# Five groups computed plainly and two pairs by seven products, instead of three and three, in a linear-attention and gated-MLP kernel

## The chip, the cores and the metric

The kernel runs on one core of one Trainium2 chip. The metric is the device time of one execution in microseconds. Three executions of the kernel before took 922.75, 929.16 and 931.92 us, median 929.16 us.

## What is computed

Inputs q, k and v have the shape 8 batches x 8 heads x 576 positions x 64, and `w_in` is 512 x 2048 and `w_out` 2048 x 512, all float32. The reference is:

```python
q_s = softmax(q, axis=-1); k_s = softmax(k, axis=2)      # sums + 1e-9
kv = np.einsum('bhsd,bhse->bhde', k_s, v)
x  = np.einsum('bhsd,bhde->bhse', q_s, kv)               # -> 4608 x 512
h  = x @ w_in                                            # 4608 x 2048
out = (h * np.cos(h)) @ w_out                            # 4608 x 512
```

## The kernel before, in words

**Tokens.** The 576 positions of each batch are cut into 512 and 64. The first 512 of batch b are group b (0 to 7); the eight remainders of 64 together are group 8. So the MLP runs over nine groups of 512 tokens, and over 16 blocks f of 128 columns of `w_in`.

**Precision.** A float32 operand is split into a high and a low part of a reduced type, and a product is three matmuls: high x high, high x low, low x high. A first-layer result h of one group and one f (128 x 512) therefore takes 4 chunks x 3 = 12 matmuls of 128x128 by 128x512 (`unit1`, L839), and the second layer of one group and one f takes 4 row blocks x 3 = 12 more, added into four `acc` banks (`unit2`, L923). Between the two stand the gating, h*cos(h), in four steps (`gated`: turns on ACT L864, rest on DVE L868, cos on ACT L874, gate on DVE L879), and the split of the result (`split_g`: ACT L895, DVE L899). The first six units use plain float32 in the second layer (L916).

**Plain groups and pairs.** Groups below `std` (3) are computed this plain way, 16 units each; the rest, (3,4), (5,6) and (7,8), are taken in pairs by a seven-product scheme (`pair`, `block`, L1152). For a pair and two neighbouring f, the four results (two groups x two f) come from seven products of 6 matmuls each, instead of 4 x 12 = 48 matmuls. The scheme needs sums and differences of x (`x_sums`: L1064, L1075, L1079) and of the weights (`sums`: L998 to L1009, computed once, written to the DRAM tensor `w_sums`, and loaded again for each block of each pair by four GpSimd DMAs, L1127). Within a block the products go to two PSUM banks, `z` and `a` (products 0, 2, 4, 6 to z; 1, 3, 5 to a), and intermediate sums are copied and added into SBUF cells `c` by ACT (L1166) and DVE (L1173). Only the last product's result is gated straight from the bank z.

**PSUM.** There are eight banks: h x 2, acc x 4, att x 2. In a plain group h alternates between the two h banks. In a block z alternates between the two h banks from block to block, and `a` is always the bank `att` 1.

**Attention.** It goes by batch b and by pairs p of heads (`k_steps`: the kv product, L599; `q_steps`; `x_steps`: two matmuls of 128x128 by 128x288 in plain float32, L712, into two banks `xo`). For b below `std` the two use both att banks, and x stays in SBUF (ACT L726 and L729, DVE L737). From `std` on, `spare()` gives `att` 0 alone, since `a` lives in `att` 1: both matmuls go to the same bank, each is copied by ACT (`x_row`, L742) into one row buffer `xs`, and the row is written to the DRAM tensor `x_main`, from which `x_sums` loads it. The softmax steps that matter below are the exponentials on ACT (`q_exp` L653, `k_exp` L561). Exp and sin need different activation tables, each loaded by an instruction on ACT.

**Order.** Nothing waits by hand. `Plan` collects every step with its engine, its assumed duration, what it reads and writes and a due time; `order()` list-schedules them (ACT, DVE, PE, POOL, SP, and the buses of the DMAs) and the instructions are issued on each engine's queue in the order found. The engines then run in order, and semaphores follow from the data. `CFG["spans"]` says over which units of the plain groups the attention of a later batch is to be spread; `CFG["tables"]` = 0 means that the planner gives table loads no time. SP issues all plain DMAs, GpSimd the loads of `w_sums`.

Of the kernel before, what the change touches and what calls it, by code (L numbers as in the profile page):

```python
# [43 lines left out]
    att1=(5.98, 6.97),  # L44
    std=3,
    spans={2: (15.0, 28.0), 3: (24.0, 38.0), 4: (32.0, 47.0)},
    phi=0.906,
# [9 lines left out]
    rounds=8,  # L57
    tables=0,
    alpha=1.33,
# [3 lines left out]
class Plan:  # L63
# [6 lines left out]

    LAT = {("POOL", "SWB"): 0.3, ("ACT", "PE"): 0.37, ("DVE", "PE"): 0.3, ("DVE", "ACT"): 0.14, ("DVE", "DVE"): 0.13,
           ("PE", "PE"): 0.07, ("SP", "SP"): 0.0, ("SP", "BUS"): 0.2}

    def __init__(self):
        self.steps = []
        self.writer, self.readers = {}, {}

    def add(self, eng, us, fn, reads=(), writes=(), due=None, table=None, after=0.0):
# [18 lines left out]
    def load(self, us, fn, reads=(), writes=(), due=None, after=0.0, parts=1, seq=()):  # L97

        t = object()
        self.add(  # L100
            "SP", 0.65 * parts, fn, reads=reads, writes=[*writes, t, *seq], due=due, after=after
        )
        self.add("BUS", us, None, reads=[*reads, t], writes=writes)

    def cast_load(self, us, fn, reads=(), writes=(), due=None):

        t = object()
        self.add("POOL", 1.1, fn, reads=reads, writes=[*writes, t], due=due)
        self.add("SWB", us, None, reads=[*reads, t], writes=writes)

    def lat(self, i, j):

        a, b = self.steps[i], self.steps[j]
        return self.LAT.get((a[0], b[0]), 1.0 if a[0] in ("BUS", "SWB") else 0.2)

    def run(self, edges, prio, release=None, tables=False):
# [14 lines left out]
        for _ in range(n):  # L131
            best = None
            for e in engines:
                if can[e]:
                    t = free[e]
                elif wait[e]:
                    t = max(free[e], wait[e][0][0])
                else:
                    continue
                if best is None or t < best[0]:  # L140
                    best = (t, e)
            t, e = best
            w, c = wait[e], can[e]
            while w and w[0][0] <= t:
                at, i = heappop(w)
                heappush(c, (at if e in ("BUS", "SWB") else prio[i], i))
# [57 lines left out]
def linear_attention_then_cos_gated_mlp(  # L204
# [18 lines left out]
    nc = tc.nc  # L223
# [47 lines left out]
    def v_frame(t):  # L271
# [17 lines left out]
    w_rows = dr.tile([NF, P, DM], F32, name="w_rows")  # L289
    w_sums = dr.tile([NF // 2, P, 7, 2, 2 * P], F32, name="w_sums")  # L290

# [4 lines left out]
    BUFS = dict(  # L296
        x4k=8, kq=2, qm=1, qs=2, ql=1, mt=1, m1=1, m=2, r=2, kvw=4, xs=1, stage=2, wc=2, r2=3, ghi=2,
        glo=2, h=2, acc=4, att=2, qb=1, qf=2, qd=2, sr=5, c=4,
    )
# [18 lines left out]
    for tag, size in (  # L318
# [4 lines left out]
        ("r2", TB), ("ghi", TB), ("glo", TB), ("stage", TB), ("wc", 2 * DM),  # L323
        ("kvw", P), ("mt", 4 * P), ("m1", 2 * P), ("m", 2 * P), ("xs", S), ("kq", 4 * NC * D), ("qb", S), ("qf", S),
    ):
# [255 lines left out]
    def spare(tag, b):  # L581

        return ring(tag) if tag != "att" or b < CFG["std"] else (tag, 0)

# [89 lines left out]
    def x_steps(b, p, place, kvw, tq, tx, due_q, due_x):  # L674
# [7 lines left out]
        slot = ring("x4k") if keep else None  # L682
        xr, xs = quarters(slot), ring("xs")
        cols = [slice(0, HALF), slice(HALF, TB)]
# [89 lines left out]
        cold = 2.0 if b == 0 and p < CFG["cold"] else 1.0  # L774
        qf = ring("qf")
        if blocks:
# [209 lines left out]
    def sums(n):  # L986

        f = 2 * n
        s, hs, ls = ring("wc"), ("x4k", 2 + 2 * (n % 2)), ("x4k", 3 + 2 * (n % 2))

# [16 lines left out]
        def lo():  # L1007
            t = T["sl", n] = sbt([P, 2 * DM], F32R, ls, f"sl_{n}")
            nc.vector.tensor_sub(  # L1009
                t, T["sum", n].rearrange("p f d -> p (f d)"), T["sh", n].bitcast(F32)  # L1010
            )

        def put(i):
            t = T["sh" if i == 0 else "sl", n].bitcast(F32).rearrange("p (s d) -> p s d", s=4)
# [8 lines left out]
        plan.load(0.73 * 2, rows, reads=[("rows", f), ("rows", f + 1)], writes=[s])  # L1023
        plan.add("DVE", 1.5, adds, writes=[s])
        plan.add("ACT", 1.1, hi, reads=[s], writes=quarters(hs))
        plan.add("DVE", 1.22, lo, reads=[s, *quarters(hs)], writes=quarters(ls))
        plan.load(1.0, lambda: put(0), reads=quarters(hs), writes=[("sums", n, 0)], parts=2)
        plan.load(1.0, lambda: put(1), reads=quarters(ls), writes=[("sums", n, 1)], parts=2)
        plan.load(
            2.2, own, reads=[("w", "i", f), ("w", "i", f + 1)], writes=[("sums", n, 2)], parts=3,  # L1030
            due=when(20 + 2.5 * n),
        )


    ORDER = ("11", "5", "6", "3", "7", "2", "4")
    XAT = {0: (2, 3), 1: (4, 5), 6: (6, 7)}
# [10 lines left out]
    def x_sums(k, b1, b2):  # L1047
# [6 lines left out]
        for c in range(2):  # L1054
# [34 lines left out]
            for i, m, sub in (  # L1089
                (0, A0, None),  # L1090
                (1, A0, (A0, A1, A0)),
                (2, A0, (A0, B1, A0)),
                (3, B1, None),
                (4, A1, (A1, B1, A1)),
                (5, B0, None),
                (6, B0, (B0, B0, A0)),
# [6 lines left out]
                xp = x_places(i, c)  # L1103
                plan.add("ACT", 0.62, lambda i=i, m=m, hi=hi: hi(i, m), reads=at(m) + [st[m[0]]], writes=xp)
                plan.add("DVE", 0.69, lambda i=i, m=m, lo=lo: lo(i, m), reads=at(m) + [st[m[0]]], writes=xp)
# [6 lines left out]
    def block(k, n, b1, b2, flip, due):  # L1112

        z, aux = ring("h"), ("att", 1)
        c1, c5, c2 = (ring("c") for _ in range(3))
# [3 lines left out]
        for m in range(4):  # L1119
            place = wide(ring("sr")[1])  # L1120

            def load(m=m, place=place):
                e = min(2 * m + 2, 7)
                t = sbt([P, e - 2 * m, 2, 2 * P], F32R, f"wi{place[2]}", f"s_{k}_{n}_{m}")
                for i in range(2 * m, e):
                    T["s", k, n, i] = t[:, i - 2 * m]
                nc.gpsimd.dma_start(t, w_sums[n, :, 2 * m : e])  # L1127

            plan.cast_load(
                2.0 if m < 3 else 1.2, load, reads=[("sums", n, i) for i in range(3)],  # L1130
                writes=[place, (place, 0), (place, 1)],
# [25 lines left out]
        def pe(i, to, first=False):  # L1157
            plan.add(
                "PE", us, lambda: product(i, to, first),
                reads=[*x_places(i, 0), *x_places(i, 1), ws[i // 2]],  # L1160
                writes=[z if to == "z" else aux], due=due + i * us * CFG["phi"],
            )
# [47 lines left out]
        pe(5, "a", True)  # L1210
        add("a", c1)
        G[b1, f] = post(2, b1, f, c1)
        pe(6, "z")
# [139 lines left out]
    for u in range(NU + 2):  # L1353
        if u >= 2:
            unit2(u - 2, order[u - 2], G.pop(u - 2), when(u + 0.4))
        if u < NU:
            b, f = order[u][:2]
            prepare("i", f)
            if b not in X:
# [57 lines left out]
```

## Time and profile before

| what | value |
|---|---|
| three executions | 922.75, 929.16, 931.92 us |
| profiled execution | 923.85 us, of which the span from the first to the last instruction is 921.8 us |
| granted TensorE clock, mean | 0.987 of full speed |
| busy: PE, PEld, DVE, ACT, POOL | 859.0, 677.9, 617.6, 546.0, 88.6 us |
| first-layer matmuls of plain groups (L839) | 576, from 37.7 to 352.5 us |
| matmuls of the seven-product blocks (L1152) | 1008, from 357.3 to 891.4 us |

Busy times are sums over the span; an engine's share says nothing of which wait ends last, so idle times with their releasers and stretches of the timeline are needed beside them. A matmul's own duration (389 ns for 128x512) is longer than the distance to the next one in a row, because matmuls are pipelined; the pace is read from rows that merge several.

### The profile page before, as it was taken

What the parts mean: (1) busy time and instruction counts of PE and PEld (TensorE: products, weight loads), DVE (VectorE), ACT (ScalarE), POOL (GpSimd) and SP (SyncE); (2) the same over time, 40 slices, a digit from 0 to 9 for tenths busy, and PEclk for the clock granted to TensorE, in tenths of its full rate; (3) what the DMA queues carried; (4) which work ended last, traced back from release to release, by engine and by line L of the source; (5) the groups of instructions that cost most, each with busy time, mean ns of one, the idle gap of its engine ahead of it and who ended that gap; (6) DMA issues with size and microseconds to landing.
All of it is one profiled execution on the core that took longest, in us unless ns stands there. A gap on an engine that the chain in (4) does not pass through costs nothing.

```text
span 921.8 us, 12171 instructions
## 1 busy us (share of the span) xinstructions
PE 859.0 (93%) x4144; PEld 677.9 (74%) x4144; DVE 617.6 (67%) x995; ACT 546.0 (59%) x910; POOL 88.6 (10%) x181
## 2 busy tenths in 40 slices
PE   6889999999898989889899989979999999999998
PEld 4556777877676777668687768757788788878876
DVE  7778889978666967678266757875345666534552
ACT  3798797766555565666446665754445655543541
POOL 1200100100100002012001101100000011100100
PEclk8799999999999999999999999999999999999999
DMA  8993599828579874697349457866324447342312
GB/s 216 340 281 126 170 349 269 229 79 225 131 245 291 204 230 120 178 241 193 120 104 240 121 188 198 212 149 150 101 81 126 148 140 215 101 130 74 98 31 83
DMA packets 209981, 159.67 MB, mean 173 GB/s; under 512 B 115200, under 2 KB 176128, under 8 KB 209920
## 3 DMA queue, kind: packets, MB, share of 16 engines
q1 hardware_dynamic: 196096, 114.86, 44.8%
q0 software_dynamic: 13824, 44.05, 17.6%
q8 instruction: 33, 0.54, 0.2%
q14 instruction: 28, 0.23, 0.1%
HBM read 111.94 MB, written 46.92 MB: 172 GB/s over the span
## 4 chain that ended last, share of the span: by engine, by line
PE 48%; DMA 9%; ACT 6%; DVE 5%; issue 4%; SPq 3%; POOL 0%; ACTq 0%; DVEq 0%; POOLq 0%
PE acc L923 25%; PE z L1152 10%; PE a L1152 7%; PE h L839 4%; DMA q<-in_q_dram 3%; PE x_False L712 2%; DMA s<-w_sums 1%; DMA out_dram<-o 1%; SPq L490 1%; SPq L486 1%; PE kv L599 1%; ACT xs L742 1%; DMA w_sums<-sl 1%; DVE xs L1079 1%; DVE qm L646 1%
## 5 line engine op out<-in xcount | busy, mean ns | idle before, releaser
L1152 PE MATMUL z<-xs,s 128*128 128x512 f32 x576 | 148.3, 395 | 3.0 <-DVE kt L879 1.0
L839 PE MATMUL h<-x,w_i 128*128 128x512 f32 x576 | 143.8, 399 | 4.7 <-DVE kt L879 3.3
L839 PEld LDWEIGHTS h<-x,w_i 128*128 128x128 f32 x576 | 107.4, 189 | 30.7 <-DVE kt L879 5.5
L1152 PEld LDWEIGHTS z<-xs,s 128*128 128x128 f32 x576 | 108.1, 189 | 27.9 <-DVE c L1173 2.5
L1152 PE MATMUL a<-xs,s 128*128 128x512 f32 x432 | 113.2, 398 | 4.6 <-ACT c L1166 4.0
L923 PE MATMUL acc<-w_o,ghi 128*128 128x512 f32 x336 | 108.1, 403 | 1.7 <-DVE o L961 1.1
L1152 PEld LDWEIGHTS a<-xs,s 128*128 128x128 f32 x432 | 81.5, 190 | 23.5 <-ACT c L1166 5.0
L1127 POOL DMA_DIRECT2D s<-w_sums x96 | 50.9, 531 | 415.4 <-PE a L1152 271.2
L923 PEld LDWEIGHTS acc<-w_o,ghi 128*128 128x128 f32 x336 | 62.3, 188 | 16.4 <-DVE o L961 1.9
L712 PE MATMUL x_False<-qf,kvw 128*128 128x288 f32 x128 | 45.6, 444 | 28.7 <-ACT xs L742 24.4
L923 PE MATMUL acc<-w_o,glo 128*128 128x512 f32 x168 | 65.8, 391 | 0.4 <-DVE glo L899 0.4
L712 PEld LDWEIGHTS x_False<-qf,kvw 128*128 128x128 f32 x128 | 22.7, 197 | 43.3 <-ACT xs L742 32.9
L1173 DVE TENSOR_TENSOR c<-a,c 128x512 f32<-128x512 f32 x48 | 33.1, 689 | 22.6 <-PE a L1152 22.2
L864 ACT ACTIVATE stash<-c 128x512 int32<-128x512 f32 x36 | 22.7, 632 | 39.5 <-DVE c L1173 39.2
L864 ACT ACTIVATE kt<-h 128x512 int32<-128x512 f32 x48 | 28.5, 594 | 29.0 <-PE h L839 26.5
L1166 ACT COPY c<-z 128x512 f32<-128x512 f32 x48 | 28.1, 586 | 25.7 <-PE z L1152 25.4
L868 DVE SCALAR_TENSOR_TENSOR kt<-kt,h 128x512 f32<-128x512 int32 x48 | 32.6, 681 | 11.3 <-ACT kt L864 11.3
L874 ACT ACTIVATE kt<-kt 128x512 f32<-128x512 f32 x48 | 30.3, 633 | 15.9 <-DVE kt L868 15.5
L874 ACT ACTIVATE stash<-stash 128x512 f32<-128x512 f32 x48 | 30.3, 631 | 13.5 <-DVE stash L868 13.4
L646 DVE TENSOR_REDUCE qm<-q 128x18 f32<-128x1152 f32 x16 | 21.6, 1350 | 24.4 <-DMA q<-in_q_dram 24.4
L879 DVE TENSOR_TENSOR kt<-kt,h 128x512 f32<-128x512 f32 x42 | 28.6, 680 | 13.6 <-ACT kt L874 13.4
L923 PEld LDWEIGHTS acc<-w_o,glo 128*128 128x128 f32 x168 | 31.5, 188 | 7.7 <-DVE glo L899 0.9
(872 smaller groups left out, 1763.3 us busy)
## 6 DMA issues: line engine op xcount, KB each, us to landing
s<-w_sums POOLq DMA_DIRECT2D x72, 512.0 KB, 4.4
q<-in_q_dram SPq DMA_DIRECT2D x32, 256.0 KB, 5.4
raw_i<-in_moe_w_in_dram SPq DMA_DIRECT2D x16, 512.0 KB, 5.9
raw_o<-in_moe_w_out_dram SPq DMA_DIRECT2D x16, 512.0 KB, 6.4
out_dram<-o SPq DMA_DIRECT2D x32, 256.0 KB, 2.9
v_sb<-in_v_dram SPq DMA_DIRECT2D x30, 256.0 KB, 4.4
k<-in_k_dram SPq DMA_DIRECT2D x14, 512.0 KB, 5.2
qb<-q_rows SPq DMA_DIRECT2D x96, 72.0 KB, 3.2
```

Of the source, the lines that this page charges most:

```text
L646: nc.vector.tensor_reduce(out=m, in_=rows(), axis=AX.X, op=ALU.max)
L712: nc.tensor.matmul(t[:, 0:HALF], T["kv", b, p], T["qf", b, p][:, cs], start=True, stop=not again)
L839: nc.tensor.matmul(o, a, x, start=(c == 0 and n == 0), stop=(c == KC - 1 and n == 2))
L864: nc.scalar.activation(t.bitcast(I32), src(), AF.Identity, bias=0.25, scale=1.0 / TWO_PI)
L868: nc.vector.scalar_tensor_tensor(t, t.bitcast(I32), -TWO_PI, src(), op0=ALU.mult, op1=ALU.add)
L874: nc.scalar.activation(t, t, AF.Sin, bias=0.5 * math.pi)
L879: nc.vector.tensor_mul(o, t, src())
L923: nc.tensor.matmul(T["acc", j], a[:, js], w, start=(first and n == 0), stop=(last and n == 2))
L1127: nc.gpsimd.dma_start(t, w_sums[n, :, 2 * m : e])
L1152: nc.tensor.matmul(o, a, x, start=(first and c == 0 and m == 0), stop=(c == 1 and m == 2), skip_group_check=not first,)
L1166: "ACT", 0.6, lambda: nc.scalar.copy(cell(place), T["z" + to, k, n]),
L1173: lambda: nc.vector.tensor_add(cell(place), T["z" + to, k, n], cell(place)),
```

## The change

`std` becomes 5: groups 0 to 4 are plain, and the pairs are (5,6) and (7,8). The attention of each batch is spread over other units, up to batch 6. `spare()` gives both att banks to all batches, and the blocks use the two h banks alone: z in h bank n % 2 and `a` in the other. The products are issued in the order 0, 5, 2, 1, 4, 3, 6, with the loads of their weights regrouped to match. `w_sums` holds only the four sums; the unchanged parts of `w_in` are kept in a second tensor `w_own`. The low parts of the sums are computed in place. The row buffers `qf` x 2 and `xs` become one ring `row` x 3. The planner gives a table load its time, counts DMAs from batch 2 on 1.3 times as long, and treats GpSimd's loads as users of the same bus as the others.

```diff
 CFG = dict(
-    std=3,
-    spans={2: (15.0, 28.0), 3: (24.0, 38.0), 4: (32.0, 47.0)},
+    std=5,
+    slow=1.3,
+    spans={2: (15.0, 28.0), 3: (29.0, 42.0), 4: (43.0, 56.0), 5: (52.0, 66.0), 6: (62.0, 77.0)},
...
-    tables=0,
+    tables=1.0,
...
-    w_sums = dr.tile([NF // 2, P, 7, 2, 2 * P], F32, name="w_sums")
+    w_sums = dr.tile([NF // 2, P, 4, 2, 2 * P], F32, name="w_sums")
+    w_own = dr.tile([NF, P, 2, DM], F32, name="w_own")
...
     def spare(tag, b):
-        return ring(tag) if tag != "att" or b < CFG["std"] else (tag, 0)
+        return ring(tag)
...
-        xr, xs = quarters(slot), ring("xs")
+        xr = quarters(slot)
...
-        qf = ring("qf")
+        qf, xs = ring("row"), ring("row")
...
     def sums(n):
-        s, hs, ls = ring("wc"), ("x4k", 2 + 2 * (n % 2)), ("x4k", 3 + 2 * (n % 2))
+        s, hs = ring("wc"), ("x4k", 2 + n % 4)
+        due = when((CFG["std"] - 1) * NF + 1.7 * n)
...
-            nc.sync.dma_start(w_sums[n, :, 2:5, i], t[:, 0:3])
-            nc.sync.dma_start(w_sums[n, :, 1, i], t[:, 3])
-
-        def own():
-            for x, k, at in ((f, 0, 0), (f, 1, 5), (f + 1, 1, 6)):
-                t = T["w", "i", x].bitcast(F32)
-                nc.sync.dma_start(w_sums[n, :, at], t[:, :, k * 2 * P : (k + 1) * 2 * P])
+            nc.sync.dma_start(w_sums[n, :, :, i], t)
+
+        def own(x, k):
+            nc.sync.dma_start(w_own[x, :, :, k * 2 * P :], T["w", "i", x].bitcast(F32)[:, :, k * 2 * P :])
...
-    ORDER = ("11", "5", "6", "3", "7", "2", "4")
+    ORDER = (0, 5, 2, 1, 4, 3, 6)
+    TILE = (0, 1, 1, 2, 2, 0, 3)
...
     def block(k, n, b1, b2, flip, due):
-        z, aux = ring("h"), ("att", 1)
+        z, aux = ("h", n % 2), ("h", 1 - n % 2)
...
         pe(0, "z", True)
         copy("z", c1)
+        pe(5, "a", True)
+        add("a", c1)
+        G[b1, f] = post(2, b1, f, c1)
+        pe(2, "z")
+        copy("z", c2)
         pe(1, "a", True)
         copy("a", c5)
-        pe(2, "z")
-        copy("z", c2)
+        pe(4, "z")
+        add("z", c5)
+        G[b2, f + 1] = post(1, b2, f + 1, c5)
         pe(3, "a")
         add("a", c2)
         G[b2, f] = post(0, b2, f, c2)
-        pe(4, "z")
-        add("z", c5)
-        G[b2, f + 1] = post(1, b2, f + 1, c5)
-        pe(5, "a", True)
-        add("a", c1)
-        G[b1, f] = post(2, b1, f, c1)
         pe(6, "z")
         G[b1, f + 1] = post(3, b1, f + 1, z)
...
-            if u == 2 * NF:
+            if u == (STD - 1) * NF:
                 for n in range(NF // 2):
                     sums(n)
```

## Rows read from the trace of the kernel before

**Rows 1.** The page: busy us of each engine, share of the span, instructions.

```profile
PE 859.0 (93%) x4144; PEld 677.9 (74%) x4144; DVE 617.6 (67%) x995; ACT 546.0 (59%) x910; POOL 88.6 (10%) x181
```

**Rows 2.** PE's waits, whole span: waiting line, releaser, total us, times, longest.

```profile
PE x_False L712 <- ACT xs L742: 24.4, 20, 2.9
PE a L1152 <- ACT c L1166: 4.0, 2, 3.1
PE h L839 <- DVE kt L879: 3.3, 4, 1.6
PE acc L923 <- ACT o L964: 2.3, 4, 0.9
PE kv L599 <- DMA v_sb<-in_v_dram: 1.4, 1, 1.4
PE z L1152 <- DVE kt L879: 1.0, 1, 1.0
```

**Rows 3.** Stretches: busy us of PE, PEld, DVE, ACT, POOL, then PEclk, DMA share, GB/s.

```profile
248.20:352.70 104.50, 94.30 (x465) 73.52 (x463) 74.78 (x121) 56.99 (x88) 5.31 (x13) 1.00 0.79 227
772.00:890.00 118.00, 117.23 (x517) 96.68 (x517) 62.08 (x95) 57.06 (x97) 10.56 (x20) 1.00 0.34 96
```

**Rows 4.** The chain of waits: a first-layer unit; one product of a block.

```profile
350.14 2.73 PE h L839 x12
419.21 1.36 PE z L1152 x6
```

**Rows 5.** Timeline of PE, two attention matmuls of batch 5: start us, us.

```profile
406.65 0.65 PE L712 MATMUL x_False<-qf,kvw 128*128 128x288 f32 x2
406.92 0.85 PE L923 MATMUL acc<-w_o,ghi_('s', 0, 0, 3)_3693 128*128 128x512 f32 x2
...
412.98 0.75 PE L712 MATMUL x_False<-qf,kvw 128*128 128x288 f32 x2 [2.92 <-ACT xs L742]
413.35 1.76 PE L1152 MATMUL z<-xs,s 128*128 128x512 f32 x6
```

**Rows 6.** Timeline of ACT across the same wait.

```profile
409.15 1.28 ACT L653 ACT_TABLE_LOAD   x1
410.44 1.16 ACT L653 ACTIVATE q<-q 128x1152 f32<-128x1152 f32 x1
411.51 0.61 ACT L864 ACTIVATE kt_('s', 0, 2, 2)_3858<-c 128x512 int32<-128x512 f32 x1
...
412.54 0.39 ACT L742 COPY xs<-x_False 128x288 f32<-128x288 f32 x1
```

**Rows 7.** Timeline of PE, attention of batch 2, which has both banks.

```profile
172.55 1.13 PE L712 MATMUL x_False<-qf,kvw 128*128 128x288 f32 x4
173.31 3.15 PE L839 MATMUL h<-x,w_i 128*128 128x512 f32 x12
```

**Rows 8.** Timeline of PE and DVE: last product, then z's gate, blocks 0, 7, 19, 23.

```profile
377.61 2.88 PE L1152 MATMUL z<-xs,s 128*128 128x512 f32 x12
390.99 0.69 DVE L879 TENSOR_TENSOR kt_('s', 0, 0, 3)_3619<-kt_('s', 0, 0, 3)_3619,z 128x512 f32<-128x512 f32 x1 [2.15 <-ACT kt_('s', 0, 0, 3)_3619 L874]
...
549.64 1.52 PE L1152 MATMUL z<-xs,s 128*128 128x512 f32 x6
565.33 0.68 DVE L879 TENSOR_TENSOR stash<-stash,z 128x512 f32<-128x512 f32 x1
...
802.40 1.52 PE L1152 MATMUL z<-xs,s 128*128 128x512 f32 x6
805.98 0.69 DVE L879 TENSOR_TENSOR kt_('s', 2, 3, 3)_6957<-kt_('s', 2, 3, 3)_6957,z 128x512 f32<-128x512 f32 x1 [0.70 <-ACT kt_('s', 2, 3, 3)_6957 L874]
...
890.22 1.52 PE L1152 MATMUL z<-xs,s 128*128 128x512 f32 x6
894.29 0.69 DVE L879 TENSOR_TENSOR stash<-stash,z 128x512 f32<-128x512 f32 x1 [1.19 <-ACT stash L874]
```

**Rows 9.** Groups by line: ACT's largest group of table loads.

```profile
L874 ACT ACT_TABLE_LOAD x26 | 33.4, 1283 | 0.5
```

More of the change, by code (lines that the diff above doesn't have):

```diff
@@ L63 @@
 class Plan:
-    LAT = {("POOL", "SWB"): 0.3, ("ACT", "PE"): 0.37, ("DVE", "PE"): 0.3, ("DVE", "ACT"): 0.14, ("DVE", "DVE"): 0.13,
+    LAT = {("POOL", "BUS"): 0.5, ("ACT", "PE"): 0.37, ("DVE", "PE"): 0.3, ("DVE", "ACT"): 0.14, ("DVE", "DVE"): 0.13,
            ("PE", "PE"): 0.07, ("SP", "SP"): 0.0, ("SP", "BUS"): 0.2}
@@ L76, in __init__ @@
         self.writer, self.readers = {}, {}
+        self.slow = 1.0
     def add(self, eng, us, fn, reads=(), writes=(), due=None, table=None, after=0.0):
@@ L100, in load @@
         self.add(
-            "SP", 0.65 * parts, fn, reads=reads, writes=[*writes, t, *seq], due=due, after=after
+            "SP", 0.65 * self.slow * parts, fn, reads=reads, writes=[*writes, t, *seq], due=due, after=after
         )
-        self.add("BUS", us, None, reads=[*reads, t], writes=writes)
+        self.add("BUS", self.slow * us, None, reads=[*reads, t], writes=writes)
     def cast_load(self, us, fn, reads=(), writes=(), due=None):
         t = object()
-        self.add("POOL", 1.1, fn, reads=reads, writes=[*writes, t], due=due)
-        self.add("SWB", us, None, reads=[*reads, t], writes=writes)
+        self.add("POOL", 0.6, fn, reads=reads, writes=[*writes, t], due=due)
+        self.add("BUS", self.slow * us, None, reads=[*reads, t], writes=writes)
     def lat(self, i, j):
         a, b = self.steps[i], self.steps[j]
-        return self.LAT.get((a[0], b[0]), 1.0 if a[0] in ("BUS", "SWB") else 0.2)
+        return self.LAT.get((a[0], b[0]), 1.0 if a[0] == "BUS" else 0.2)
     def run(self, edges, prio, release=None, tables=False):
@@ L145, in run @@
                 at, i = heappop(w)
-                heappush(c, (at if e in ("BUS", "SWB") else prio[i], i))
+                heappush(c, (at if e == "BUS" else prio[i], i))
             i = heappop(c)[1]
@@ L296, in linear_attention_then_cos_gated_mlp @@
     BUFS = dict(
-        x4k=8, kq=2, qm=1, qs=2, ql=1, mt=1, m1=1, m=2, r=2, kvw=4, xs=1, stage=2, wc=2, r2=3, ghi=2,
-        glo=2, h=2, acc=4, att=2, qb=1, qf=2, qd=2, sr=5, c=4,
+        x4k=8, kq=2, qm=1, qs=2, ql=1, mt=1, m1=1, m=2, r=2, kvw=4, row=3, stage=2, wc=2, r2=3, ghi=2,
+        glo=2, h=2, acc=4, att=2, qb=1, qd=2, sr=5, c=4,
     )
@@ L323, in linear_attention_then_cos_gated_mlp @@
         ("r2", TB), ("ghi", TB), ("glo", TB), ("stage", TB), ("wc", 2 * DM),
-        ("kvw", P), ("mt", 4 * P), ("m1", 2 * P), ("m", 2 * P), ("xs", S), ("kq", 4 * NC * D), ("qb", S), ("qf", S),
+        ("kvw", P), ("mt", 4 * P), ("m1", 2 * P), ("m", 2 * P), ("row", S), ("kq", 4 * NC * D), ("qb", S),
     ):
@@ L1007, in lo @@
         def lo():
-            t = T["sl", n] = sbt([P, 2 * DM], F32R, ls, f"sl_{n}")
-            nc.vector.tensor_sub(
-                t, T["sum", n].rearrange("p f d -> p (f d)"), T["sh", n].bitcast(F32)
-            )
-        def put(i):
-            t = T["sh" if i == 0 else "sl", n].bitcast(F32).rearrange("p (s d) -> p s d", s=4)
-            nc.sync.dma_start(w_sums[n, :, 2:5, i], t[:, 0:3])
-            nc.sync.dma_start(w_sums[n, :, 1, i], t[:, 3])
-        def own():
-            for x, k, at in ((f, 0, 0), (f, 1, 5), (f + 1, 1, 6)):
-                t = T["w", "i", x].bitcast(F32)
-                nc.sync.dma_start(w_sums[n, :, at], t[:, :, k * 2 * P : (k + 1) * 2 * P])
@@ L1023, in sums @@
[L1023 to L1032, printed above, removed]
@@ L1035, in linear_attention_then_cos_gated_mlp, with put @@
-    ORDER = ("11", "5", "6", "3", "7", "2", "4")
+            t = T["sum", n].rearrange("p f d -> p (f d)")
+            nc.vector.tensor_sub(t, t, T["sh", n].bitcast(F32))
+        def put(i):
+            if i == 0:
+                t = T["sh", n].bitcast(F32).rearrange("p (s d) -> p s d", s=4)
+            else:
+                t = T["sum", n].rearrange("p f (k d) -> p (f k) d", k=2)
+            nc.sync.dma_start(w_sums[n, :, :, i], t)
+        def own(x, k):
+            nc.sync.dma_start(w_own[x, :, :, k * 2 * P :], T["w", "i", x].bitcast(F32)[:, :, k * 2 * P :])
@@ new lines, in sums @@
+        plan.load(0.73 * 2, rows, reads=[("rows", f), ("rows", f + 1)], writes=[s], due=due)
+        plan.add("DVE", 1.8, adds, writes=[s])
+        plan.add("ACT", 1.1, hi, reads=[s], writes=quarters(hs))
+        plan.add("DVE", 1.22, lo, reads=quarters(hs), writes=[s])
+        plan.load(1.46, lambda: put(0), reads=quarters(hs), writes=[("sums", n, 0)])
+        plan.load(1.46, lambda: put(1), reads=[s], writes=[("sums", n, 1)])
+        for k in range(2):
+            plan.load(
+                1.46 - 0.73 * k, lambda k=k: own(f + k, k), reads=[("w", "i", f + k)], writes=[("own", f + k)],
+                due=when((CFG["std"] - 2.5 + 0.18 * n) * NF),
+            )
@@ L1090, in x_sums @@
                 (0, A0, None),
+                (5, B0, None),
                 (1, A0, (A0, A1, A0)),
                 (2, A0, (A0, B1, A0)),
+                (4, A1, (A1, B1, A1)),
                 (3, B1, None),
-                (4, A1, (A1, B1, A1)),
-                (5, B0, None),
                 (6, B0, (B0, B0, A0)),
@@ L1103, in x_sums @@
                 xp = x_places(i, c)
-                plan.add("ACT", 0.62, lambda i=i, m=m, hi=hi: hi(i, m), reads=at(m) + [st[m[0]]], writes=xp)
+                plan.add(
+                    "ACT", 0.62, lambda i=i, m=m, hi=hi: hi(i, m), reads=at(m) + [st[m[0]]],
+                    writes=xp + [("xw", i)],
+                )
                 plan.add("DVE", 0.69, lambda i=i, m=m, lo=lo: lo(i, m), reads=at(m) + [st[m[0]]], writes=xp)
@@ L1122, in load @@
             def load(m=m, place=place):
[L1123 to L1127, printed above, removed]
+                shape = ([P, 2, DM], [P, 2, 2, 2 * P], [P, 2, 2, 2 * P], [P, 2, 2 * P])[m]
+                t = sbt(shape, F32R, f"wi{place[2]}", f"s_{k}_{n}_{m}")
+                if m == 0:
+                    T["s", k, n, 0], T["s", k, n, 5] = t[:, :, 0 : 2 * P], t[:, :, 2 * P : DM]
+                    src = w_own[f]
+                elif m == 3:
+                    T["s", k, n, 6] = t
+                    src = w_own[f + 1, :, :, 2 * P : DM]
+                elif m == 1:
+                    T["s", k, n, 2], T["s", k, n, 1] = t[:, 0], t[:, 1]
+                    src = w_sums[n, :, 0:4:3]
+                else:
+                    T["s", k, n, 3], T["s", k, n, 4] = t[:, 0], t[:, 1]
+                    src = w_sums[n, :, 1:3]
+                nc.gpsimd.dma_start(t, src)
             plan.cast_load(
-                2.0 if m < 3 else 1.2, load, reads=[("sums", n, i) for i in range(3)],
+                1.8 if m < 3 else 1.0, load,
+                reads=[("sums", n, 0), ("sums", n, 1)] if m in (1, 2) else [("own", f + m // 3)],
                 writes=[place, (place, 0), (place, 1)],
@@ L1159, in pe @@
                 "PE", us, lambda: product(i, to, first),
-                reads=[*x_places(i, 0), *x_places(i, 1), ws[i // 2]],
-                writes=[z if to == "z" else aux], due=due + i * us * CFG["phi"],
+                reads=[*x_places(i, 0), *x_places(i, 1), ws[TILE[i]]],
+                writes=[z if to == "z" else aux], due=due + ORDER.index(i) * us * CFG["phi"],
             )
@@ L1357, in linear_attention_then_cos_gated_mlp @@
             b, f = order[u][:2]
+            if b == 2:
+                plan.slow = CFG["slow"]
             prepare("i", f)
```

## The prediction, made before the changed kernel was run

> **What bounds the kernel now.** I read the page first, then PE's waits, then stretches and the timeline around the longest waits. The page shows TensorE busy for 93% of the span, and the next engine, DVE, for 67% [rows 1]. The stretch 772 to 890 us, in the last pair and without any attention, is what that looks like undisturbed: PE is busy for 117.2 of 118.0 us while DVE and ACT need 62 and 57 us [rows 3]. So work added to PE costs its full duration, and work taken from DVE, ACT or the DMA queues costs or gives nothing unless PE waits for it.
>
> Where PE does wait, one cause outweighs the rest: the attention's second matmul waits for ACT to copy out the first, 24.4 us in 20 waits; every other cause in the list is 4.0 us or less [rows 2]. The 20 are the five batches 3 to 7, which share one bank, times four head pairs. The timeline shows one. The first matmul (two records, as plain float32 takes two passes there) runs at 406.65 us, a full second-layer pass follows, and then PE stands 2.92 us until the copy is done [rows 5]. ACT was not working on that copy: a table load, an exponential and two steps of the gating stood ahead of it in its queue [rows 6]. In batch 2, with two banks, the two matmuls run together as four records and PE goes on at once [rows 7].
>
> **The change part by part**, against the profiled execution's 923.85 us (span 921.8 us). That execution is 0.6% below the median of the three shown, 929.16 us; the sum stands against the 923.85.
>
> *One pair less by seven products.* Two plain groups have 2 x 16 x 12 = 384 first-layer matmuls, a pair 8 x 7 x 6 = 336. The second layer is the same. A run of 12 takes 2.73 us and one of 6 takes 1.36 us [rows 4], so 0.227 us each, and 48 more cost **+10.9 us**. All of it is on PE, and PE sets the end; no engine can hide it.
>
> *Two banks for the attention.* `spare()` now alternates the banks for every batch, so the second matmul no longer needs the first one's copy. The 24.4 us go: **-24.4**. Around each wait PE also loses a little on changing over. With one bank, 406.65 to 413.35 is 6.70 us; less the second-layer pass between (12 matmuls, 2.72) and the wait (2.92), 1.06 us are left for both matmuls [rows 5]. With two banks both take 172.55 to 173.31, 0.76 us [rows 7]. That is 0.30 us a time, 6.0 us in 20; I take **-5**, with ends 0 and -6. Late next is only the release of the bank for the next head pair, and batch 2 shows no wait for it there.
>
> *More plain stretch in place of the pair.* The plain stretch of group 2, 248.2 to 352.7 us, is the nearest row for groups 3 and 4: PE is busy 94.3 of 104.5 us, with DVE at 75, ACT at 57 and the DMA share at 0.79 [rows 3]. Its waits other than the copies are the gate, the output and a late v load, 1.9 + 0.7 + 1.4 = 4.0 us, parts of the totals in [rows 2]. Two more such stretches bring at most +8. The pair that goes takes little away, since the waits of its beginning (up to 3.1 us for a copy to c, 1.0 us for a gate) come back at the beginning of (5,6). This stretch also holds all of `sums` now, which the change spreads over the last two groups. I take **+3**, ends 0 and +8.
>
> *One bank fewer for the products.* A block's `a` is the bank that held the z of the block before. Product 5, now second, cannot start before the last z has been gated. The gate ends 2.75 us after the end of the last product at best (803.92 to 806.67, block 19) and 14.8 us after it at worst (551.16 to 566.01, block 7); from the first of the 24 blocks (380.49 to 391.68) to the last (891.74 to 894.98) the middle value is 4.1 us [rows 8]. Cover is product 0 of the next block, 1.36 us, and a second-layer pass of 2.72 us [rows 4], 4.08 us together, and each block brings four passes. Where the late gates stand, nothing was waiting for them. With two pairs there are 15 such boundaries. If the planner always puts a pass there, this costs nothing; if never, 15 x (2.75 - 1.36) = 21 us. I take **+2**, close to the lower end because the planner sees the bank and the passes are there.
>
> *Table loads with a time.* A load is 1.283 us, 26 of them for the sine alone [rows 9], and the old plan gave them none, so ACT ran behind its plan. The waits that a truer order could save are those for copies, outputs and gates, 4.0 + 2.3 + 3.3 + 1.0 = 10.6 us [rows 2]. I take **-4**, ends -10 and +5, as another order can also be a worse one. The exponential begins 0.01 us after its load [rows 6], so 1.28 us is all it costs. The Trainium skill, ScalarE: Activation LUTs, section What ACT_TABLE_LOAD costs, adds about 1.38 us of drain to each switch, which would leave the new plan's ACT too fast as well and this term near 0, the sum near 910; the trace disagrees, and the measurement decides.
>
> *The remaining edits*, 0 together, ends -2 and +3: the order of products and weight tiles, `w_own`, `sums` in place, the ring of three rows. `w_own` takes 16 writes instead of 24, `put` 16 instead of 32, and 16 transfers of `x_main` and their issues go from SP's queue; a third of the loads of `w_sums` (32 of 96) go from GpSimd's. What `sums` issues is moved past the attention loads of batches 5 and 6 on SP's queue instead of those of 3 and 4, which are the same transfers. All that is covered by PE's matmuls; without that cover it would show as a wait on a load like the 1.4 us of the late v now [rows 2]. The three rows let xs be filled while the last one is still being written out. The removed `x_sums` of one pair is DVE and ACT work beside PE, and counts nothing.
>
> Sum: 923.85 + 10.9 - 24.4 - 5 + 3 + 2 - 4 = **906.4 us**. The ends of the terms give 892 (10.9 - 24.4 - 6 + 0 + 0 - 10 - 2) and, with the products' bank at half its price and the others at their dear ends, 926.
>
> **Rivals.** *The wait moves to the products' bank (slower).* Place: product 5 of each block, until the gate of the block before. Price: were each gate only as early as the median now, and the planner put no pass ahead of it, 4.1 - 1.36 = 2.7 us at 15 boundaries, 41 us instead of 2: **945 us**. It decides above (923.85 - 904.4) / 15 = 1.3 us a boundary, and slower by over 1% comes above 1.9. For it: gates are late today, and exponentials with their table loads stand ahead in ACT's queue while batch 7's attention runs. Against it: 15 times four passes can fill the place, and ACT is half idle in [rows 3]. The Trainium skill's Perfetto Trace Analysis, section Matmuls, asks that independent groups rotate through different banks so that evacuation overlaps the next group; that speaks for the attention's half of this change and against the products' half. Chance 0.09.
>
> *The time is given back.* The copies go, but ACT is as late as before, so PE waits a moment later for something else in the same queue, such as a copy to c; or the bank costs its 1.39 us per boundary. With half of 29 us given back, or the 21 us instead of 2: **921 to 925 us**. For it: in [rows 6] the two gating steps ahead of the copy feed PE too. Against it: PE's other waits for ACT are small although ACT is equally late for them. Chance 0.20.
>
> *More comes back than I counted.* All the waits for ACT and for gates go with the truer plan, and the new plain stretches run without their own: the sum without +3 and +2 and with -10: **895 us**. For it: the stretch from 772 us runs almost without waits. Against it: plain stretches had waits beside the attention's. Chance 0.15.
>
> *The change does not do what it says*: the two matmuls would still land on one bank. The ring's calls for the two follow each other, so they always differ; 0.01, at 923.85 + 10.9 = 935 us.
>
> **How the numbers follow.** The forecast, 906 us, has 0.55. A change within 1% (9 us) can't be told from none here: the limits are 915 and 933. Faster by over 1%: the forecast but for 0.03 at its dear end, the larger gain (0.15), and 0.03 of the case of time given back, which reaches down to 912: 0.70. Within 1%: the rest of that case and the dear end, 0.20. Slower: the products' bank and the last rival, 0.10. The range from 892 to 925 leaves out these two, 0.05 of the larger gain below 892 and 0.03 of the time given back above 925, together 0.18.
>
> **What would show it.** L1152 should have 672 matmuls and L839 960; the wait of x_False for the copies to xs should be gone or under 3 us; the attention matmuls of batches 3 to 7 should come as four records together, as in batch 2; a plain group should take about 95 to 98 us (16 x 5.44 = 87 us of units, 7 us of attention and its waits). New waits of `a` on a DVE gate would show the rival of the bank, at over 20 us in sum. A sum of PE's waits as large as now, with other names, would show that the time was given back. The forecast is wrong if PE's idle time after 40 us is not at least 20 us less than now.

## The result, and the profile after

The changed kernel takes 879.0 us (median of four executions, 877.9 to 879.24) against 928.75 us before: a ratio of 0.947, interval 0.942 to 0.952. The prediction had the direction, but a fall of 17.5 us where 45 (profiled executions) to 50 us (medians) came; the time lies below the range. The profiled execution took 879.14 us, its span is 877.3 us, 44.5 less than before.

The page after, to be set beside [rows 1]: busy us of each engine, then PE's busy tenths in 40 slices.

```profile
PE 855.6 (98%) x4192; PEld 689.8 (79%) x4192; DVE 596.9 (68%) x961; ACT 523.3 (60%) x878; POOL 77.9 (9%) x149
PE   6889999999999999999999999999999999999998
```

All waits of PE from 37.7 to 870 us, to be set beside [rows 2] (the copies' 24.4 us have no row left, nor have late v loads):

```profile
PE kv L602 <- ACT kvw L622: 2.1, 1, 2.1
PE acc L926 <- ACT o L967: 1.2, 2, 0.9
PE kv L602 <- ACT k L564: 1.2, 1, 1.2
PE z L1170 <- DVE kt L882: 0.5, 1, 0.5
PE a L1170 <- DVE kt L882: 0.4, 1, 0.4
PE h L842 <- DVE kt L882: 0.2, 1, 0.2
```

The work itself is as forecast. Groups by line, with count, busy us, mean ns and idle time of PE's matmuls; the last two rows are the attention's matmuls before and after:

```profile
L842 PE MATMUL h<-x,w_i 128*128 128x512 f32 x960 | 236.2, 397 | 0.2 <-DVE kt L882 0.2
L1170 PE MATMUL z<-xs,s 128*128 128x512 f32 x384 | 97.8, 392 | 0.5 <-DVE kt L882 0.5
L1170 PE MATMUL a<-xs,s 128*128 128x512 f32 x288 | 73.9, 392 | 0.4 <-DVE kt L882 0.4
L712 PE MATMUL x_False<-qf,kvw 128*128 128x288 f32 x128 | 45.6, 444 | 28.7 <-ACT xs L742 24.4
L715 PE MATMUL x_False<-qf,kvw 128*128 128x288 f32 x128 | 40.2, 430 | 2.8 <-ACT kvw L622 2.8
```

Stretches, busy us of PE, PEld, DVE, ACT and POOL, then granted clock, DMA share and GB/s: first the kernel before, from its first unit to the last matmul, then the same of the kernel after and its groups 2, 3 and 4.

```profile
37.70:918.00 880.30, 833.32 (x3996) 658.47 (x3994) 588.09 (x919) 527.02 (x869) 81.03 (x160) 1.00 0.61 169
```

```profile
37.70:873.60 835.90, 830.25 (x4044) 670.03 (x4042) 569.93 (x888) 505.79 (x840) 68.72 (x128) 1.00 0.55 153
239.40:339.40 100.00, 100.00 (x502) 81.38 (x501) 66.75 (x109) 57.82 (x94) 7.90 (x18) 1.00 0.39 94
339.40:433.10 93.70, 93.70 (x542) 76.05 (x542) 59.06 (x95) 58.45 (x93) 4.53 (x11) 1.00 0.46 117
433.10:527.00 93.90, 93.31 (x441) 76.03 (x439) 69.70 (x112) 55.27 (x88) 5.90 (x12) 1.00 0.71 212
```

PE stands idle for 880.30 - 833.32 = 47.0 us before and 835.90 - 830.25 = 5.7 us after. That is 41.3 of the 44.5 us. PE's busy time falls by 3.1 us although it holds 10.9 us more of matmuls, so 14 us went from it too. The attention's matmuls account for some 5 of them (45.6 to 40.2 us over the whole span). The granted clock is 1.00 in both stretches and does not account for the rest; the likely cause is the running out and in around the waits that are gone (45 before and 7 after in the lists) and pauses too short to be listed, but no run shows it apart. -41.3 + 10.9 - 14 = -44.4 us. A plain group with its attention now runs almost without a pause: PE is idle for 0.0, 0.0 and 0.6 us in groups 2, 3 and 4, against 10.2 us in group 2 before [rows 3].

Of the signs that the prediction named, the counts (672 and 960) and the missing wait for the copies came as written; the two matmuls of a head pair run together in 7 of the 8 pairs of batches 3 and 4, but only in 6 of the 12 of batches 5 to 7, with other matmuls between them in the rest; groups 3 and 4 take 93.7 and 93.9 us instead of 95 to 98 (the working given for it, 87 + 7, adds to 94); and PE's idle time fell by 41 us where at least 20 were asked. The sign of the four records was read from one pair: in batch 2 of the kernel before only the pair of [rows 7] ran so, and the other three stand 3 to 11 us apart.

### The profile page after: what moved, and what is told of

The parts are those of the page before. It is cut to its first block, busy times and chain, and to the rows that moved or that the text cites. A ratio compares the mean times of both kernels' runs of the same rounds, so it can differ in the third digit from the quotient of the medians.

```text
span 877.3 us, 12066 instructions
## 1 busy us (share of the span) xinstructions
PE 855.6 (98%) x4192; PEld 689.8 (79%) x4192; DVE 596.9 (68%) x961; ACT 523.3 (60%) x878; POOL 77.9 (9%) x149
## 4 chain that ended last, share of the span: by engine, by line
PE 93%; DMA 2%; SPq 2%; ACT 2%; DVE 1%; issue 0%; ACTq 0%
PE acc L926 42%; PE h L842 25%; PE z L1170 10%; PE a L1170 7%; PE x_False L715 4%; PE acc L919 2%; PE kv L602 2%; DMA x_left<-xl 1%; DMA raw_i<-in_moe_w_in_dram 1%; SPq L493 0%; PE qt L694 0%; SPq L489 0%; DVE kt L871 0%; PE x_True L715 0%; SPq L474 0%
## 5 line engine op out<-in xcount | busy, mean ns | idle before, releaser
L842 PE MATMUL h<-x,w_i 128*128 128x512 f32 x960 | 236.2, 397 | 0.2 <-DVE kt L882 0.2
L842 PEld LDWEIGHTS h<-x,w_i 128*128 128x128 f32 x960 | 180.8, 190 | 40.6 <-DVE kt L882 0.8
L926 PE MATMUL acc<-w_o,ghi 128*128 128x512 f32 x592 | 187.8, 398 | 0.0
L926 PEld LDWEIGHTS acc<-w_o,ghi 128*128 128x128 f32 x592 | 110.3, 188 | 24.0
L926 PE MATMUL acc<-w_o,glo 128*128 128x512 f32 x296 | 115.5, 390 | 0.0
L1170 PE MATMUL z<-xs,s 128*128 128x512 f32 x384 | 97.8, 392 | 0.5 <-DVE kt L882 0.5
L1170 PEld LDWEIGHTS z<-xs,s 128*128 128x128 f32 x384 | 71.9, 188 | 16.0 <-DVE kt L882 0.9
L898 ACT CAST ghi<-kt 128x512 fp32r<-128x512 f32 x74 | 45.7, 618 | 49.9 <-PE acc L926 47.5
L1170 PE MATMUL a<-xs,s 128*128 128x512 f32 x288 | 73.9, 392 | 0.4 <-DVE kt L882 0.4
L902 DVE TENSOR_TENSOR glo<-kt,ghi 128x512 fp32r<-128x512 f32 x74 | 51.1, 690 | 31.1 <-ACT ghi L898 30.8
L1170 PEld LDWEIGHTS a<-xs,s 128*128 128x128 f32 x288 | 53.9, 188 | 12.2 <-DVE kt L882 0.5
L715 PE MATMUL x_False<-qf,kvw 128*128 128x288 f32 x128 | 40.2, 430 | 2.8 <-ACT kvw L622 2.8
L602 PEld LDWEIGHTS kv<-v_sb,k 128*64 128x64 f32 x600 | 21.1, 146 | 15.9 <-issue 8.6
```

The lines of the kernel that those rows point to most:

```text
L602: nc.tensor.matmul(x[h * D : (h + 1) * D, odd : odd + vt.shape[1]], t[:, h, c, :], vt, start=(c == CM), stop=(c == CM - 1),)
L715: nc.tensor.matmul(t[:, 0:HALF], T["kv", b, p], T["qf", b, p][:, cs], start=True, stop=not again)
L842: nc.tensor.matmul(o, a, x, start=(c == 0 and n == 0), stop=(c == KC - 1 and n == 2))
L898: nc.scalar.copy(t, T["g", u])
L902: nc.vector.tensor_sub(t, T["g", u], T["gh", u].bitcast(F32))
L926: nc.tensor.matmul(T["acc", j], a[:, js], w, start=(first and n == 0), stop=(last and n == 2))
```

## The experiments

Each time is the median of four executions, each ratio is against the kernel before on the same chip: 929.65 us beside runs 1 to 4, 926.24 beside 5 to 8, 927.89 beside 9 to 12 and 928.70 beside 13 to 16. PE's idle time is given from 37.7 us to its last matmul, as above: 47.0 us before, 5.7 after. Three theories are told apart. **A**: the 20 waits for the copies were outside the plan, and pushed what followed off it. **B**: table loads without a time made the other waits. **C**: the third pair's DVE, ACT and DMA work made them.

**1. One bank, but the copy where it belongs in the plan.** In the kernel before both matmuls of a head pair are declared ahead of both copies. With one bank for both, the planner then takes the first copy to depend on the second matmul, while on the chip the second matmul needs the first copy. So ACT gets the copy behind work that the plan puts ahead of the second matmul, as in [rows 6].

```diff
         for i in range(2):
             plan.add("PE", us, lambda i=i: x_mm(i), reads=[qf, kvw], writes=[xo[i]], due=due_x)
-        if not keep:
-            for i in range(2):
+            if not keep:
                 plan.add("ACT", 0.4, lambda i=i: x_row(i), reads=[xo[i]], writes=[xs])
+        if not keep:
```

> The kernel before with one bank as before, only the order of the declared steps changed: matmul, copy, matmul, copy instead of both matmuls and then both copies, so that the planner knows that the second matmul needs the first copy. Theory A (the wait was outside the plan, and it pushed everything behind it off the plan): the waits of x_False for the copies fall from 24.4 us to under 8, PE's other waits after 40 us shrink as well, and the time is 880 to 892 us. Theory B (the other waits came from table loads that the plan gave no time): only the waits for the copies and their change-over go, 24 to 30 us: 894 to 900 us. Theory C (the third pair's own DVE, ACT and DMA work made the other waits): as B, 894 to 900 us.

907.1 us, ratio 0.978 (0.973 to 0.983). PE's waits after 37.7 us: the three largest, and those for the copies.

```profile
PE a L1152 <- DVE c L1173: 8.2, 3, 3.9
PE kv L599 <- DMA v_sb<-in_v_dram: 4.8, 2, 3.0
PE x_False L712 <- DVE qf L771: 2.9, 3, 1.1
PE x_False L712 <- ACT xs L742: 1.3, 2, 0.7
```

The copies' waits fall from 24.4 to 1.3 us with one bank. The others do not shrink but come under other names: PE's idle time is 29.5 us, so 28.2 without the copies, against 22.6 before. A is right about the copies and wrong about the rest. The gain is less than any theory had.

**2. And table loads with a time**, on top of run 1.

```diff
-    tables=0,
+    tables=1.0,
```

> As the run before in this call, and the planner gives table loads their time (tables = 1.0). Theory A: within 5 us of that run, at 878 to 892 us. Theory B: 12 to 20 us less than that run, about 880 us. Theory C: no change, 894 to 900 us.

909.9 us, 0.979 (0.974 to 0.985), PE idle for 29.9 us: no difference from run 1. B fails here.

**3. The changed kernel with three pairs.**

```diff
-    std=5,
+    std=3,
     slow=1.3,
-    spans={2: (15.0, 28.0), 3: (29.0, 42.0), 4: (43.0, 56.0), 5: (52.0, 66.0), 6: (62.0, 77.0)},
+    spans={2: (15.0, 28.0), 3: (24.0, 38.0), 4: (32.0, 47.0)},
```

> The changed kernel with three pairs again (std = 3 and the old spans), everything else as changed: two attention banks, shared product banks, table loads planned. Theories A and B: PE stays without waits and saves the 48 matmuls, 879 - 10.9 = 868 us, up to 872. Theory C: the waits of the third pair come back, 15 to 25 us, and the time is 883 to 895 us.

887.0 us, 0.954 (0.953 to 0.956). The 10.9 us of matmuls are saved, and 19 us come back, 13.6 of them idle time of PE (19.3 us against 5.7). Its longest waits after 37.7 us:

```profile
PE kv L602 <- DMA v_sb<-in_v_dram: 5.4, 1, 5.4
PE h L842 <- DVE g L882: 3.5, 1, 3.5
PE acc L926 <- DVE o L964: 3.4, 1, 3.4
```

C holds within the changed kernel.

**4. The changed kernel without time for table loads.**

```diff
-    tables=1.0,
+    tables=0,
```

> The changed kernel with tables = 0: the planner gives table loads no time, as before. Theory A: 879 to 885 us. Theory B: most of the 24 us that I had not counted come back, 893 to 903 us. Theory C: 879 to 882 us.

889.0 us, 0.957 (0.955 to 0.959): 10 us more, in the range of neither A nor B, with 12.2 us of idle time. New beside the kernel after are 4.6 us of h waiting for a gate and 3.5 us for g:

```profile
PE h L842 <- DVE kt L882: 4.6, 3, 2.5
PE h L842 <- DVE g L882: 3.5, 1, 3.5
```

**5 and 6. The changed kernel with one bank for batches 5 to 7**, first with the old declaration, then with that of run 1.

```diff
     def spare(tag, b):
-        return ring(tag)
+        return ring(tag) if tag != "att" or b < CFG["std"] else (tag, 0)
```

> The changed kernel, but the attention of batches 5 to 7 goes through one bank, with both matmuls declared before both copies, as in the kernel before. If the planner's wrong order of matmul and copy was what cost the 24 us, its 12 waits come back at 1.2 to 1.6 us each: 893 to 899 us. If the waits came from a lack of planned table time or from the third pair, fewer and shorter ones come back: 880 to 887 us.

> As the run before in this call, one bank for batches 5 to 7, but declared matmul, copy, matmul, copy. If the order in the plan was the cost and not the number of banks: 879 to 883 us, with x_False waiting under 3 us. If the second bank itself is what helps: 890 us or more.

Run 5 takes 898.8 us, 0.969 (0.966 to 0.973), and run 6 takes 882.2 us, 0.951 (0.948 to 0.954). The two differ in the place of the copy's declaration alone. In run 5 PE's largest wait is this, and in run 6 the copies have no row at all:

```profile
PE x_False L715 <- ACT xs L745: 9.5, 11, 1.3
```

So the second bank is worth 3 us here, no more than two orders of one kernel differ by (runs 13 and 14). What cost the time was the order in the plan: 16.5 us for 12 head pairs, 1.4 us each, of which 0.8 are listed as waits. In run 6 a first-layer unit, a second-layer pass or a product stands between the two matmuls of each of the 12 pairs, so that the copy runs beside it. PE's timeline of one pair:

```profile
402.98 0.65 PE L715 MATMUL x_False<-qf,kvw 128*128 128x288 f32 x2
403.25 3.15 PE L842 MATMUL h<-x,w_i 128*128 128x512 f32 x12
406.23 0.65 PE L715 MATMUL x_False<-qf,kvw 128*128 128x288 f32 x2
```

The Trainium skill, Perfetto Trace Analysis, section Matmuls, asks that independent groups of matmuls rotate through different banks so that the evacuation of one overlaps the next. In run 6 the overlap is there with one bank, since other groups go to other banks in between, and a second bank adds nothing that these runs can tell.

**7. The changed kernel without the factor on transfers in the plan.**

```diff
-    slow=1.3,
+    slow=1.0,
```

> The changed kernel with slow = 1.0, so that the planner gives DMAs their old length after batch 2. If what the gain had beyond my sum came from fewer pairs: 878 to 883 us. If it came from transfers planned early enough: waits on v loads, on qf and on o come back, 886 to 897 us.

886.2 us, 0.956 (0.953 to 0.959), 7 us more. The time fits the second expectation; of the waits it named only those on o grew, to 3.5 us from 1.2. PE is idle for 13.1 us, against 5.7 to 8.0 in the changed kernel and its two other orders (runs 13 and 14); the slowest of these is 3 us away, so part of the 7 can be the order.

**8. Two pairs with the rest of before**, on top of run 2.

```diff
-    std=3,
+    std=5,
-    spans={2: (15.0, 28.0), 3: (24.0, 38.0), 4: (32.0, 47.0)},
+    spans={2: (15.0, 28.0), 3: (29.0, 42.0), 4: (43.0, 56.0), 5: (52.0, 66.0), 6: (62.0, 77.0)},
```

> The kernel before with the copy planned and table loads planned, as the second run, and with five plain groups and two pairs (std = 5 and the new spans); banks of the products, product order, sums, row buffers and the length of DMAs as before. If the third pair's work made the remaining waits, 20 to 30 us of them go against 10.9 us of matmuls: 885 to 900 us. If the remaining edits (DMA lengths, row buffers, sums, product order) removed them, the pair less brings its matmuls alone: 910 to 920 us.

909.5 us, 0.981 (0.977 to 0.985). The pair less costs 10.9 us and gives back the same, no more. PE is idle for 28.2 us, and one place holds 10 of them. PE's timeline, idle time and releaser in brackets:

```profile
261.98 0.72 PE L712 MATMUL x_False<-qf,kvw 128*128 128x288 f32 x2 [1.69 <-DVE qf L771]
267.31 1.33 PE L712 MATMUL x_False<-qf,kvw 128*128 128x288 f32 x2 [4.60 <-ACT kvw L619]
272.41 8.12 PE L839 MATMUL h<-x,w_i 128*128 128x512 f32 x24 [3.78 <-DVE kt L879]
```

DVE's just then:

```profile
266.98 0.42 DVE L998 TENSOR_TENSOR sum<-sum 128x256 f32<-128x256 f32 x1 [2.38 <-DMA sum<-w_rows]
...
269.96 0.42 DVE L998 TENSOR_TENSOR sum<-sum 128x256 f32<-128x256 f32 x1
...
271.67 0.68 DVE L879 TENSOR_TENSOR kt<-kt,h 128x512 f32<-128x512 f32 x1
```

and ACT's last cosines before that gate:

```profile
265.58 1.15 ACT L874 ACTIVATE kt<-kt 128x512 f32<-128x512 f32 x2
```

The cosine was there at 266.73 us at the latest, but in DVE's queue the gate (L879) for which PE was waiting stood behind other work: DVE stood 2.38 us for the rows of the weight sums, did two lots of sums with a softmax reduction between them, and only then the gate. So the late load is 2.4 of the 3.78 us at most; the rest is the sums standing ahead. The whole stretch, and the part around the waits, in which the DMA share is 1.02 and the granted clock 0.69:

```profile
240.00:284.00 44.00, 31.83 (x123) 24.25 (x122) 34.43 (x58) 19.89 (x28) 0.64 (x3) 0.84 1.03 300
262.00:284.00 22.00, 13.62 (x45) 10.14 (x46) 17.11 (x29) 10.10 (x16) 0.34 (x2) 0.69 1.02 300
```

**9. Run 8 with the sums spread over the last plain group.**

```diff
-        plan.load(0.73 * 2, rows, reads=[("rows", f), ("rows", f + 1)], writes=[s])
+        plan.load(0.73 * 2, rows, reads=[("rows", f), ("rows", f + 1)], writes=[s], due=when((CFG["std"] - 1) * NF + 1.7 * n))
...
-            if u == 2 * NF:
+            if u == (STD - 1) * NF:
```

> The run with the old rest and two pairs (909.5 us), with one thing more: the sums of w_in are computed during the last plain group, 1.7 units apart, instead of at the beginning of group 2. If that bunch of DVE and DMA work caused the 16 us that PE lost there from 240 to 283 us: 892 to 900 us. If the loss only moves with the sums: 905 to 912 us.

897.5 us, 0.967 (0.964 to 0.971), 12 us less than run 8, with 21.1 us of idle time. The edit both moves the sums to a later group and sets them apart; which of the two counts was not tried. The same stretch, now undisturbed:

```profile
240.00:284.00 44.00, 44.00 (x226) 35.62 (x225) 30.14 (x52) 24.63 (x45) 3.92 (x9) 1.00 0.44 118
```

**10. The changed kernel with the old row buffers.**

```diff
-        x4k=8, kq=2, qm=1, qs=2, ql=1, mt=1, m1=1, m=2, r=2, kvw=4, row=3, stage=2, wc=2, r2=3, ghi=2,
+        x4k=8, kq=2, qm=1, qs=2, ql=1, mt=1, m1=1, m=2, r=2, kvw=4, qf=2, xs=1, stage=2, wc=2, r2=3, ghi=2,
...
-        qf, xs = ring("row"), ring("row")
+        qf, xs = ring("qf"), ring("xs")
```

> The changed kernel with the row buffers of before, qf x 2 and xs x 1 instead of one ring of three. If a lone xs made copies wait for the write of the row before: 883 to 890 us. If nobody waits for that: 878 to 882 us.

884.3 us, 0.953 (0.949 to 0.956), with 11.0 us of idle time. PE's new waits are for a low part of the gated result (3.6 us), a v load (2.8 us) and a low part of x (1.9 us), none for rows. That is 1 us above run 13 below, so this is inconclusive.

**11. Three pairs, the work before them spread**, on top of run 3.

```diff
-    spans={2: (15.0, 28.0), 3: (24.0, 38.0), 4: (32.0, 47.0)},
+    spans={2: (15.0, 28.0), 3: (22.0, 35.0), 4: (30.0, 43.0)},
...
-        due = when((CFG["std"] - 1) * NF + 1.7 * n)
+        due = when((CFG["std"] - 1) * NF + 1.2 * n)
```

> The changed kernel with three pairs, as the third run (887 us), with the attention of batches 3 and 4 two and four units earlier and the sums 1.2 units apart. If crowding just before the first pair is what a third pair costs and it can be spread: 870 to 878 us, less than the changed kernel. If the plain stretch is too short for the work in any order: 884 to 892 us.

890.3 us, 0.959 (0.956 to 0.963), with 21.0 us of idle time: no better than run 3.

**12. Run 9 with transfers from batch 2 on planned 1.3 times as long.**

```diff
+        self.slow = 1.0
...
-            "SP", 0.65 * parts, fn, reads=reads, writes=[*writes, t, *seq], due=due, after=after
+            "SP", 0.65 * self.slow * parts, fn, reads=reads, writes=[*writes, t, *seq], due=due, after=after
...
-        self.add("BUS", us, None, reads=[*reads, t], writes=writes)
+        self.add("BUS", self.slow * us, None, reads=[*reads, t], writes=writes)
...
+            if b == 2:
+                plan.slow = 1.3
```

> The first run of this call (old rest, two pairs, sums spread), with DMAs from batch 2 on planned 1.3 times as long. If the planned length acts as in the changed kernel: 7 us less than that run, 885 to 893 us. If it helps only together with the other edits: within 3 us of that run.

889.6 us, 0.959 (0.956 to 0.962): 8 us less than run 9, about as much as in the changed kernel (run 7), with 14.4 us of idle time.

**13 to 16. Only the draw**, that is, which of many possible orders the planner happens to give. Its constant `kappa`, which changes no work and no buffer, is moved: to 1.38 and 1.42 in the changed kernel, to 1.42 in the kernel before and in that of run 3.

```diff
-    kappa=1.36,
+    kappa=1.42,
```

> The changed kernel with kappa 1.38 instead of 1.36: same work, same buffers, another order from the planner. If the changed structure is what removes the waits: 877 to 884 us. If 879 us is one lucky order: 885 us or more.

> The changed kernel with kappa 1.42, as the run before: 877 to 885 us if the structure does it, 885 us or more if 879 us is one lucky order.

> The kernel before with kappa 1.42. If its waits belong to its structure (the copy planned in the wrong place, the sums in a bunch): 920 to 936 us, the 20 waits of x_False still there at 15 us or more. If they were one unlucky order: under 915 us.

> The changed kernel with three pairs, kappa 1.42. If the third pair's waits belong to the crowded plain stretch: 883 to 895 us. If they were the draw: 868 to 878 us, faster than the changed kernel.

Run 13: 883.3 us, 0.951 (0.948 to 0.954). Run 14: 881.3 us, 0.948 (0.944 to 0.952). Run 15: 940.5 us, 1.013 (1.007 to 1.020), 4.5 us above the range expected of it. Run 16: 883.8 us, 0.951 (0.948 to 0.954). In run 15 PE's longest wait is again

```profile
PE x_False L712 <- ACT xs L742: 28.4, 20, 3.8
```

So 2 to 4 us between two orders of the changed kernel mean nothing, and in the kernel before 12 us can; 879 is the best of its three orders, not a lucky exception. The copies' waits of before belong to its structure. Three pairs, at 883.8, 887.0 and 890.3 us, come within 0.5 us of two, at 879.0 to 883.3: at equal `kappa` the pair less is worth 8.0 us (1.36) and 2.5 us (1.42), hardly more than the draw. PE's idle time does tell them apart, with 16.5 to 21.0 us for three pairs and 5.7 to 8.0 for two: what the third pair costs in waits, the 48 matmuls that it saves nearly pay for. The kernels of runs 8, 9 and 12 had one order each.

## Why the prediction was wrong in size

The sum of 906.4 us lies 27.3 us above the profiled 879.14. Of these 17.9 are idle time of PE that was not spent on the copies: it was 22.6 us before, the terms +3, +2, -4 and 0 left 23.6, and 5.7 came. Another 9 are in PE's busy time, which fell by 14 us beside the added matmuls where 5 were taken. So the steps that failed are above all the two terms for the plain stretch and for the remaining edits: they left in place waits that spreading the sums and planning longer transfers took away.

*The matmuls, +10.9*: right. Counts are 960 and 672, and the busy time agrees with the sum above.

*Two banks, -24.4 - 5*: right about the copies' waits, wrong about their cause. I took the bank as the reason and found the queue of ACT ahead of the copy [rows 6] without asking why the planner had put it there. Run 1 removes the waits with one bank (-22.6 us net); runs 5 and 6 separate the two causes in the changed kernel. As the second bank also makes the declaration right, the 24.4 came in full, and the 5 is near the 5.4 us by which the attention's matmuls fell.

*The plain stretch, +3 with ends 0 and +8*: this step failed, and its sign was wrong. I had named the spread of `sums` in it, and [rows 3] show that stretch at a DMA share of 0.79, but I read its waits as what a plain group costs. Groups 3 and 4 ran at 93.7 and 93.9 us with no more than 0.6 us idle, and group 2 lost its own waits. In the two-pair kernel the cost was the bunch of sums: the stretch from 240 to 284 us had 12.2 us of idle time with it and none without, and the time fell by 12 us (runs 8 and 9). That the 4.0 us of group 2 in the kernel before came from the sums too is likely but not shown, as no run moves the sums alone there.

*The remaining edits, 0 with ends -2 and +3*: this failed too. I looked for a wait on a DMA under its own name and found 1.4 us. But a late transfer can show as a wait for DVE, which stood behind it (2.4 us at most of one wait in run 8). Planning transfers 1.3 times as long brought 7 and 8 us (runs 7 and 12), one order each, and idle time fell by 7.4 and 6.7 us. The row buffers could not be told from the draw; product order, `w_own`, the sums in place and the planning of GpSimd's loads on the common bus were not tried alone.

*Table loads, -4 with ends -10 and +5*: -10 in the changed kernel (run 4), nothing in the kernel before with the copy planned (run 2). So the term reached its far end, and only together with other edits.

*The products' bank, +2*: nothing. PE waits for a gate at L1170 for 0.5 and 0.4 us in the whole run, so the slower rival is refuted: the bank's gate is almost never waited for.

What the rows allowed was simple, and I did not add it up. Of 47.0 us of idle time 24.4 were the copies; the other 22.6 are spread over some 25 waits of 0.2 to 3.1 us, of which [rows 2] show most of the larger. (They leave out the first 37.7 us, where two waits for k hold 5.6 us; these lie outside of this count.) I allowed for 10.6 of them at best and took 4, since no single edit named them. The chain of runs shows where time and PE's idle time went:

| kernel | time, us | PE idle, us |
|---|---|---|
| before | 928.75 | 47.0 |
| copy planned (run 1) | 907.1 | 29.5 |
| table loads planned too (run 2) | 909.9 | 29.9 |
| two pairs too (run 8) | 909.5 | 28.2 |
| sums spread too (run 9) | 897.5 | 21.1 |
| longer transfers too (run 12) | 889.6 | 14.4 |
| the rest: the changed kernel | 879.0 | 5.7 |

The last step, 10.6 us, holds the second bank (about 3 us), the row buffers (about 5 us) and edits not tried alone, and stays open in its parts, the more so as the draw is 2 to 4 us. The rival in which more comes back than counted, at 895 us, was the nearest, and its mechanism, waits that go with a truer plan, is the one that these runs show.

## What to carry to other kernels

Where a list scheduler writes the order, look first at whether it knows each buffer's true order of write, read and next write: one step declared out of place cost 20 waits, and it looks in the profile like a missing buffer. On an engine that sets the end, count all its idle time, not only the waits whose releaser the change names: a late transfer, or work queued ahead, can show under the engine that it holds up. Before crediting a few microseconds to an edit, redraw the plan with a constant that changes no work.

## What the hardware showed unexpectedly

Two long waits cost more than themselves. In run 8 the granted clock from 262 to 284 us was 0.69 of full speed. It was full before, at half, that is at 1.2 instead of 2.4 GHz, from within the wait of 4.60 us until some 5 us after the wait of 3.78 us, and then full again:

```profile
262.00:263.80 1.80, 0.70 (x2) 0.25 (x2) 1.80 (x3) 0.69 (x1) 0.00 (x0) 1.00 1.00 259
264.00:277.40 13.40, 6.32 (x14) 4.43 (x15) 10.29 (x20) 6.44 (x10) 0.20 (x1) 0.50 1.02 289
277.70:284.00 6.30, 6.30 (x30) 5.20 (x29) 4.82 (x7) 2.77 (x6) 0.13 (x1) 1.00 1.04 328
```

The 24 first-layer matmuls that began at 272.41 us took 8.12 us, against 2 x 2.73 us in [rows 4], so 2.7 us more; half of the 5 us that they ran at the low clock is 2.5.
